# Attention opening and attention-to-experts hand-over of an LSH attention + MoE kernel: transfers, weight splits and their engines re-ordered

## The chip, the cores and the metric

One core of a Trainium2 chip runs the whole program. The metric is the device time of one execution in microseconds (us), the median over several executions. The kernel before takes 697.48 us (three runs, 697.29 to 697.70).

## The reference

Attention over 4 batches x 8 heads, 768 positions, head size 64, with a mask from locality-sensitive hashing; then a mixture of 8 experts over the 3072 x 512 result, one expert per token. All is fp32.

```
q_bits = einsum(q, proj) > 0 ; k_bits = einsum(k, proj) > 0        # 6 bits per position
mask   = (bucket(q_bits)[:, None] == bucket(k_bits)[None, :])
attn   = softmax(where(mask, q @ k.T / sqrt(64), -1e9)) ; o = attn @ v
x      = o as [3072, 512]
e      = argmax(x @ w_gate)                                        # top-1 of 8
y      = softmax(x @ w_gate)[e] * sigmoid(x @ w_output_gate)[e] * (relu(x @ w1[e]) @ w2[e])
```

w1[e] is 512 x 1024 and w2[e] is 1024 x 512.

## The kernel before, in words

**Precision.** Every fp32 product is made of three fp32r products: each operand is split into a high part (a rounding copy) and a low part (operand minus high part). A split is thus a copy and a subtraction, on VectorE, ScalarE or GpSimd (DVE, ACT and POOL in the rows), of every tile that TensorE (PE) multiplies: queries and keys (`qh`, `ql`, `kh`, `kl`), weights (`w1h`, `w1l`, `w2h`, `w2l`), tokens (`xh`, `xlo`).

**Attention.** 192 steps, 12 for each of 16 pairs of heads. A step makes a tile of 128 x 768 scores (`scores`, L600 to L615), its exponentials (`soft`, L623), scales it by the inverse row sum (`normal`, L626 to L633, two steps at a time, on GpSimd), transposes it on TensorE (`transposed`, L635 to L669) and, six steps later, multiplies it with the values (`weighted`, L671 to L683). `rows` (L685 to L699) turns the result and adds the routing products. The order of all engines' work, and of the transfers that SyncE (SP) issues, is written by hand there: `plan(step, ...)` puts a piece into a step, `block(step, when, ...)` around one. `late` is step 168 of 192; late + 24 is behind the last.

**Opening.** ScalarE issues two copies: 67 columns of the projection with thresholds (`pj`, L83), and 128 columns of signs (`signs`, L87 to L91), which `signed` (L93 to L95) multiplies on GpSimd to `pjc`. SyncE loads the queries and keys of four heads (`load`, L474), 128 x 768 each: first 384 columns and last 384. While these come, TensorE turns the identity 12 times (`turn_idle`, L1044 to L1046). `first_heads` (L513 to L551) then projects head 0 to its bits (L521), splits heads 0 and 1 and compares the projections (`bt`, L530 and L502), and `spread` copies bits and queries of head 1 across partitions by transfers (`spread_half` L575, `spread_bits` L581, `spread_bits_half` L587).

**Hand-over.** The first tokens of expert 0 are gathered while the last steps run (`early_gather`, L295, two indirect transfers of GpSimd by the list `gid`), turned and split. The four pieces of expert 0's w1 (`early_load`, L1007, through `load_weights`, L156 to L183) go into raw buffers `w_raw`, of which there are two: piece 2 takes the buffer of piece 0, and piece 3 that of piece 1. `early_w1` (L1011 to L1015) splits half a piece on GpSimd. Behind the last step come the second halves of pieces 2 and 3, then w2 of expert 0 in four pieces (`w2_piece`, L1133): two are read into the spare tile `pts0` of an attention block and have their high parts made on GpSimd and their lows on VectorE; two go through `w_raw` and have their high parts made on ScalarE and their lows on GpSimd. Between them TensorE runs the last `weighted`, the first layer of expert 0 in eight pieces (`fill`, L358, with `hl` L369 on VectorE) and the routing of the last 768 tokens: `add_pair` (L735, adds the last heads' gate products, from `ot`, L683), `best` (L741), `choose` (L743, L762), `prefix` (L797 to L802).

**Later experts** read their weights through four raw buffers in turn (two `w_raw`, `xh`, `xlo`).

## Time and profile before

| | |
|---|---|
| median of three runs | 697.48 us (697.29 to 697.70) |
| the profiled execution | 696.61 us |
| its span in the trace | 694.9 us |
| TensorE (PE) busy | 683.1 us, 98% of the span |
| VectorE (DVE) busy | 460.9 us, 66% |
| ScalarE (ACT) busy | 440.0 us, 63% |
| GpSimd (POOL) busy | 417.9 us, 60% |

The span is what the trace covers of the execution; 1.7 us lie around it. Busy time does not count waits, branches and the issuing of transfers. An engine that is idle costs something only where another one waits for it. PEld is TensorE's weight load, which overlaps its matmuls; a name with a q behind it (SPq) is a queue's issuing of transfers. `[0.84 <-POOL sc L633]` at a row's end says that the engine had been idle for 0.84 us, until GpSimd's instruction of line 633 released it.

### The profile page before, as it was taken

To read this page: it belongs to the slowest core of one execution; us is meant where nothing else is said; L and a number is where in the kernel's file an instruction comes from. 1 tells how busy PE (TensorE), PEld (TensorE's weight loads), DVE (VectorE), ACT (ScalarE), POOL (GpSimd) and SP (SyncE) were. 2 spreads that over 40 slices of the span, in tenths; PEclk is the share of its full clock that TensorE was granted. 3 is DMA by queue.
4 is the path that set the end of the run, shared out by engine and by line. 5 is a ranking of instruction groups with operands and counts; after the bars stand their busy time and mean duration, and the time that the engine had idled before them with its cause. 6 is when DMAs were issued, how large, how long until landed. Compare 5 with 4: busy or idle time off the path is not lost. (4 is left out here: it accounts for less than half of the span.)

```text
span 694.9 us, 17362 instructions
## 1 busy us (share of the span) xinstructions
PE 683.1 (98%) x6591; PEld 539.3 (78%) x6591; DVE 460.9 (66%) x1012; ACT 440.0 (63%) x896; POOL 417.9 (60%) x548
## 2 busy tenths in 40 slices
PE   8999999999999999999999999999999999999996
PEld 5667676767666766666666888889999999989896
DVE  7888887888887889788876934462536354556440
ACT  5988998889888988888986224433435252434231
POOL 6767766587856678657899447163372827374201
PEclk9999999999999999999999999999999999999999
DMA  5554554364444444443444136533455444535401
GB/s 175 150 129 98 129 130 97 75 141 112 110 118 99 117 99 121 99 99 73 134 112 139 34 122 207 208 109 117 142 167 167 164 159 165 171 126 212 153 11 44
DMA packets 85283, 87.47 MB, mean 126 GB/s; under 512 B 57167, under 2 KB 67591, under 8 KB 85192
## 3 DMA queue, kind: packets, MB, share of 16 engines
q1 hardware_dynamic: 79704, 72.88, 38.5%
q0 software_dynamic: 5200, 13.31, 5.8%
q8 instruction: 54, 0.88, 0.5%
q14 instruction: 37, 0.30, 0.1%
q10 hardware_dynamic: 288, 0.10, 0.1%
HBM read 59.57 MB, written 13.11 MB: 105 GB/s over the span
## 5 line engine op out<-in xcount | busy, mean ns | idle before, releaser
L633 POOL TENSOR_SCALAR sc<-sc,rsum 128x768 f32<-128x768 f32 x192 | 171.9, 911 | 79.9 <-ACT pts L669 40.2
L615 DVE TENSOR_SCALAR_CACHE_REDUCE sc<-ps_s 128x768 f32<-128x768 f32 x192 | 176.3, 955 | 24.1 <-PE ps_s L612 22.3
L623 ACT ACTIVATE sc<-sc,mn 128x768 f32<-128x768 f32 x192 | 178.9, 951 | 3.8 <-DVE sc L615 3.7
L612 PE MATMUL ps_s<-kh,qhl 64*128 64x384 f32 x768 | 148.2, 400 | 1.4 <-DVE sc L615 0.8
L680 PE MATMUL ps_a<-pts,vt 128*64 128x384 f32 x768 | 131.2, 490 | 0.0
L669 ACT COPY pts<-ps_t 128x384 f32<-128x384 f32 x188 | 93.0, 494 | 25.3 <-PE ps_s L662 22.0
L369 DVE SCALAR_TENSOR_TENSOR hl<-ps_s,hh 128x256 fp32r<-128x256 f32 (+8 forms) x40 | 34.0, 849 | 107.6 <-ACT hh L368 107.6
L680 PEld LDWEIGHTS ps_a<-pts,vt 128*64 128x64 f32 x768 | 52.5, 137 | 66.3 <-issue 60.9
L380 POOL DMA_INDIRECT out_dram<-yo,sid x29 | 30.7, 1059 | 113.9 <-ACT yo L375 52.2
L662 PEld LDWEIGHTS ps_t<-ident,sc 64*128 64x128 f32 x1140 | 81.9, 139 | 22.1 <-POOL sc L633 13.2
L358 PE MATMUL ps_s<-xh,w1h 128*128 128x256 f32 (+7 forms) x288 | 96.8, 336 | 0.4 <-DVE hl L369 0.4
L332 POOL DMA_INDIRECT xq<-x_dram,idx x75 | 82.2, 1096 | 23.8 <-issue 21.0
L358 PE MATMUL ps_s<-xlo,w1h 128*128 128x256 f32 (+7 forms) x288 | 95.4, 331 | 0.0
L358 PE MATMUL ps_s<-xh,w1l 128*128 128x256 f32 (+7 forms) x288 | 95.3, 331 | 0.0
L662 PE MATMUL ps_t<-ident,sc 64*128 64x64 f32 x1140 | 86.9, 223 | 1.3 <-POOL sc L633 1.3
L368 ACT ACTIVATE hh<-ps_s 128x256 fp32r<-128x256 f32 (+8 forms) x40 | 29.0, 726 | 90.4 <-PE ps_s L358 90.4
L612 PEld LDWEIGHTS ps_s<-kh,qhl 64*128 64x128 f32 x768 | 76.2, 187 | 4.4 <-DVE sc L615 2.2
L612 PE MATMUL ps_s<-kl,qhl 64*128 64x384 f32 x384 | 66.6, 333 | 0.0
L612 PE MATMUL ps_s<-bb 64*128 64x384 bf16 x384 | 65.3, 327 | 0.0
L669 ACT COPY pts<-ps_m 128x384 f32<-128x384 f32 x94 | 45.1, 480 | 17.5 <-PE ps_m L662 16.1
L358 PEld LDWEIGHTS ps_s<-xh,w1h 128*128 128x128 f32 x288 | 54.2, 188 | 2.3 <-issue 0.6
L358 PEld LDWEIGHTS ps_s<-xlo,w1h 128*128 128x128 f32 x288 | 54.2, 188 | 1.4 <-DVE xlo L315 0.2
(250 smaller groups left out, 1388.4 us busy)
## 6 DMA issues: line engine op xcount, KB each, us to landing
w_raw<-in_w_dram SPq DMA_DIRECT2D x34, 512.0 KB
qk<-in_qkT_dram SPq DMA_DIRECT2D x32, 384.0 KB
qhl<-qhl SPq DMA_DIRECT2D x62, 192.0 KB
xh<-in_w_dram SPq DMA_DIRECT2D x14, 512.0 KB
xlo<-in_w_dram SPq DMA_DIRECT2D x14, 512.0 KB
vt<-in_v_dram SPq DMA_DIRECT2D x16, 384.0 KB
x_dram<-xb SPq DMA_DIRECT2D x60, 96.0 KB
xq<-x_dram,idx POOLq DMA_INDIRECT x75, 3.0
```

The costliest lines, as they stand in the source:

```text
L332: nc.gpsimd.indirect_dma_start(out=xq[:, k * P:(k + 1) * P], out_offset=None, in_=x_dram.rearrange("n (a f) -> (n a) f", a=NB32), in_offse ...
L358: nc.tensor.matmul(ps, l, r, start=first and k == 0, stop=last and k == len(pairs) - 1)
L368: nc.scalar.activation(hh, ph, AF.Relu)
L369: return lambda: nc.vector.scalar_tensor_tensor(hl, ph, 0.0, f32(hh), ALU.max, ALU.subtract)
L380: nc.gpsimd.indirect_dma_start(out=out[:, :], out_offset=bass.IndirectOffsetOnAxis(ap=sid[0:n, r, a:a + 1], axis=0), in_=yo[0:n], in_offse ...
L612: nc.tensor.matmul(ss[:, h, 0:HS], q[rs, c:c + P], k[rs, 0:HS], start=(i == 0), stop=(i == 3))
L615: nc.vector.tensor_scalar(sc, ss[:, :, 0:HS], MASKED, None, ALU.min, ALU.min, accum_out=mn)
L623: nc.scalar.activation(pr, pr, AF.Exp, bias=mn, scale=-1.0, accum_out=sums[s // GROUP][:, k, 0:1])
L633: nc.gpsimd.tensor_scalar(live[s0 + k], live[s0 + k], rs[:, k:k + 1], 0.0, ALU.mult, ALU.add)
L662: nc.tensor.transpose(trs[h][:, c], pr[r, c * P:(c + 1) * P], ident[r, r])
L669: (nc.vector.tensor_copy if h and s and (last or s % PER == 0) else nc.scalar.copy)(pts[:, :, t * P + h * hq:t * P + (h + 1) * hq], trs[h])
L680: nc.tensor.matmul(st["av"][j * D:(j + 1) * D], st["v"][:, j, c], blocks[hb][j][:, c], start=(c == 0), stop=(c == NT - 1))
```

## The change

- Opening: `pj` and the signs come in one transfer of 195 columns, issued once by ScalarE. Head 0's queries and keys come in two transfers, last 384 columns first, and the projection begins with those. VectorE makes the low queries (`ql`) ahead of the comparison `bt`. Of head 1's spreading copies, one is issued by ScalarE, and the bits' copy of the second half comes first. TensorE turns the identity 9 times, not 12.
- Last steps: the split of w1's piece 1, second half, moves from step late + 14 to late + 18, behind the gathers; piece 3 is therefore read later (late + 18 for late + 15). The first half of piece 2 has its high part copied by ScalarE. The tile of step 184 is scaled by VectorE, not GpSimd.
- Behind the last step: all four pieces of w2 are read into the two spare tiles `pts0` and `pts1`. GpSimd makes the high parts of two, ScalarE of two, VectorE all four lows. The second halves of w1's pieces 2 and 3 are split behind w2's high parts, not ahead of them.
- As w2 of expert 0 no longer takes raw buffers, each later expert's pieces fall on the four raw buffers in another turn (first `w_raw`, `w_raw`, then `xh`, `xlo`).

GpSimd's order in the hand-over (instructions of its queue from the last piece of the step before the gathers on; `w1h`, `w1l`: half a piece of w1 split; `sc`: scaling; `w2h`, `w2l`: w2 split). Before:

```order
L1014 TENSOR_SCALAR w1h<-w_raw 128x512
L1015 TENSOR_TENSOR w1l<-w_raw,w1h 128x512
L633 TENSOR_SCALAR sc<-sc,rsum 128x768 x2
L295 DMA xg<-x_dram,gid_7521 128x512 x2
L633 TENSOR_SCALAR sc<-sc,rsum 128x768 x4
...
L633 TENSOR_SCALAR sc<-sc,rsum 128x768 x6
...
L180 TENSOR_SCALAR w2h<-pts_7897 128x1024 x2
L183 TENSOR_TENSOR w2l<-w_raw,w2h 128x1024 x2
```

Of the change, on the same engine and from the same place:

```order
L634 TENSOR_SCALAR sc<-sc,rsum 128x768 x2
L289 DMA xg<-x_dram,gid_7511 128x512 x2
L634 TENSOR_SCALAR sc<-sc,rsum 128x768 x3
L1018 TENSOR_SCALAR w1h<-w_raw 128x512
L1019 TENSOR_TENSOR w1l<-w_raw,w1h 128x512 x2
L1018 TENSOR_SCALAR w1h<-w_raw 128x512
L1019 TENSOR_TENSOR w1l<-w_raw,w1h 128x512
L634 TENSOR_SCALAR sc<-sc,rsum 128x768 x6
L174 TENSOR_SCALAR w2h<-pts_7889 128x1024 x2
...
L1019 TENSOR_TENSOR w1l<-w_raw,w1h 128x512
```

One split of w1 now stands behind the gathers, one scaling and one high part have left the queue, and two low parts of w2 are gone from its end, where two splits of w1 now stand behind w2's high parts.

VectorE behind the last step (`lgt`: gate logits, `xb`: turned rows, `ot`: the last heads' result, `hl`: low part of the first layer's result). Before:

```order
L727 TENSOR_REDUCE lgt<-ps_t 128x48
L183 TENSOR_TENSOR w2l<-pts_7897,w2h 128x1024 x2
L692 STREAM_TRANSPOSE xb<-ot 128x384
L736 TENSOR_TENSOR lgt<-lgt,ps_m 128x48
L683 COPY ot<-ps_a 128x384
```

Of the change:

```order
L728 TENSOR_REDUCE lgt<-ps_t 128x48
L177 TENSOR_TENSOR w2l<-pts_7889,w2h 128x1024 x2
L177 TENSOR_TENSOR w2l<-pts_7890,w2h 128x1024 x2
L693 STREAM_TRANSPOSE xb<-ot 128x384
L737 TENSOR_TENSOR lgt<-lgt,ps_m 128x48
L684 COPY ot<-ps_a 128x384
```

Four lows of w2 instead of two now stand ahead of `ot`.

VectorE in the opening, before:

```order
L527 TENSOR_TENSOR kl<-qk,kh 128x384
L530 TENSOR_SCALAR bt<-ps_m,pj 128x384
L531 SCALAR_TENSOR_TENSOR qhl<-qk,qhl 128x384
L502 TENSOR_SCALAR bt<-ps_a,pj 64x384
L544 SCALAR_TENSOR_TENSOR qhl<-qk,qhl 64x384
```

Of the change:

```order
L522 TENSOR_TENSOR kl<-qk,kh 128x384
L524 SCALAR_TENSOR_TENSOR qhl<-qk,qhl 128x384
L527 TENSOR_SCALAR bt<-ps_m,pj 128x384
L497 TENSOR_SCALAR bt<-ps_a,pj 64x384
L539 SCALAR_TENSOR_TENSOR qhl<-qk,qhl 64x384
```

The low queries and the first comparison have changed places. The diff:

```diff
--- before.py
+++ after.py
@@ -79,20 +79,14 @@
 
 
 
-    pj = cst.tile([P, D + 3], F32, name="pj")
-    nc.scalar.dma_start(pj, proj[:, 0:D + 3])
+    pj = cst.tile([P, D + 3 + 2 * D], F32, name="pj")
+    nc.scalar.dma_start(pj, proj)
     thr, scl, set0 = (pj[:, D + i:D + i + 1] for i in range(3))
     pjc = cst.tile([P, 2, 32], F32, name="pjc")
 
-    def signs():
-
-        t = gp.tile([P, P], F32, name="t_ob")
-        nc.scalar.dma_start(t, proj[:, D + 3:])
-        return t
-
-    def signed(t):
-
-        nc.gpsimd.tensor_tensor(pjc.rearrange("p m c -> p (m c)"), t[:, 0:D], t[:, D:P], ALU.mult)
+    def signed():
+
+        nc.gpsimd.tensor_tensor(pjc.rearrange("p m c -> p (m c)"), pj[:, D + 3:2 * D + 3], pj[:, 2 * D + 3:], ALU.mult)
 
     ident = cst.tile([P, P], F32, name="ident")
     wgt = cst.tile([P, H // 2, 32], F32, name="wgt")
@@ -471,7 +465,8 @@
             st.setdefault("qk", [])
             for j in heads:
                 t = hp.tile([P, S], F32, name="qk", bufs=4)
-                nc.sync.dma_start(t, qkT[2 * g + j])
+                for c in (slice(HS, S), slice(0, HS)) if g + j == 0 else (slice(0, S),):
+                    nc.sync.dma_start(t[:, c], qkT[2 * g + j, :, c])
                 st["qk"].append(t)
 
         def load_v(g):
@@ -510,26 +505,26 @@
                 st.setdefault(k, [None, None])[j] = hp.tile([P, HS], F32R, name=k) if t is None else t
             return (st[k][j] for k in ("qk", "qh", "ql", "kh", "kl"))
 
-        def first_heads(t):
+        def first_heads():
 
             qk, qh, ql, kh, kl = tiles(0, 0)
             qk1, qh1, ql1, kh1, kl1 = tiles(0, 1)
             bb = bits_of(0, 0)
             first = slice(0, HS)
             pp = ps_m.tile([P, HS], F32, name="ps_m")
-            for m in range(2):
+            for m in (1, 0):
                 nc.tensor.matmul(pp[m * D:(m + 1) * D], pj[:, 0:D], qk[:, m * HS:(m + 1) * HS], start=True, stop=True)
             nc.scalar.copy(kh, qk[:, KEYS])
             nc.vector.tensor_scalar(qh[DOWN, KEYS], qk[UP, first], -0.125, 0.0, ALU.mult, ALU.add)
             nc.scalar.activation(qh[:, first], qk[:, first], AF.Copy, scale=-0.125)
-            signed(t)
+            signed()
             nc.gpsimd.tensor_scalar(kh1, qk1[:, KEYS], 1.0, 0.0, ALU.mult, ALU.add)
             nc.vector.tensor_tensor(kl, qk[:, KEYS], f32(kh), ALU.subtract)
             nc.scalar.activation(qh1[:, first], qk1[:, first], AF.Copy, scale=-0.125)
+            nc.vector.scalar_tensor_tensor(ql[:, first], qk[:, first], -0.125, f32(qh[:, first]),
+                                           ALU.mult, ALU.subtract)
             bt = hp.tile([P, HS], BF16, name="bt", bufs=2)
             nc.vector.tensor_scalar(bt, pp, 0.0, set0, ALU.is_gt, ALU.is_equal)
-            nc.vector.scalar_tensor_tensor(ql[:, first], qk[:, first], -0.125, f32(qh[:, first]),
-                                           ALU.mult, ALU.subtract)
             for h in range(2):
                 r = D + 32 * h
                 nc.gpsimd.tensor_scalar(bb[h * D:h * D + 2 * NB, S:S + HS], bt[r:r + 2 * NB], 1.0, 0.0,
@@ -546,7 +541,12 @@
             nc.vector.scalar_tensor_tensor(ql1[:, first], qk1[:, first], -0.125, f32(qh1[:, first]),
                                            ALU.mult, ALU.subtract)
             nc.gpsimd.tensor_tensor(kl1, qk1[:, KEYS], f32(kh1), ALU.subtract)
-            spread(0, 1)
+            spread_bits_half(0, 1, 1, nc.scalar)
+            spread_bits(0, 1, 1)
+            spread_half(0, 1, 1)
+            spread_bits(0, 1, 0)
+            spread_half(0, 1, 0)
+            spread_bits_half(0, 1, 0)
             for x in (qh, ql):
                 nc.sync.dma_start(f32(x)[UP, KEYS], f32(x)[DOWN, first])
 
@@ -580,11 +580,11 @@
             r = 32 * (2 * j + m)
             nc.sync.dma_start(bb[rows, m * S:m * S + HS], bt[r:r + 4 * NB])
 
-        def spread_bits_half(g, j, h):
+        def spread_bits_half(g, j, h, e=nc.sync):
             bt, bb = pairs[g]["bt"], bits_of(g, j)
             up = FIRST + h * 2 * NB * EVERY
             r = 64 * j + (1 - h) * 2 * NB
-            nc.sync.dma_start(bb[up:up + 2 * NB * EVERY:EVERY, HS:S], bt[r:r + 2 * NB])
+            e.dma_start(bb[up:up + 2 * NB * EVERY:EVERY, HS:S], bt[r:r + 2 * NB])
 
         def spread(g, j):
             spread_bits(g, j, 1)
@@ -630,7 +630,8 @@
             nc.vector.tensor_reduce(rs, sums.pop(s0 // GROUP), AX.X, ALU.add)
             nc.vector.reciprocal(rs, rs)
             for k in range(GROUP):
-                nc.gpsimd.tensor_scalar(live[s0 + k], live[s0 + k], rs[:, k:k + 1], 0.0, ALU.mult, ALU.add)
+                e = nc.vector if s0 + k == NSTEP - PER - GROUP else nc.gpsimd
+                e.tensor_scalar(live[s0 + k], live[s0 + k], rs[:, k:k + 1], 0.0, ALU.mult, ALU.add)
 
         def transposed(s, pr):
             g, hf, t, j = tile_of(s)
@@ -1011,7 +1012,10 @@
         def early_w1(cc, h):
             c = slice(h * F // 2, (h + 1) * F // 2)
             hi, lo, raw = (x[:, c] for x in (*early["w1"][cc], early["raw"][cc]))
-            nc.gpsimd.tensor_scalar(hi, raw, 1.0, 0.0, ALU.mult, ALU.add)
+            if (cc, h) == (2, 0):
+                nc.scalar.copy(hi, raw)
+            else:
+                nc.gpsimd.tensor_scalar(hi, raw, 1.0, 0.0, ALU.mult, ALU.add)
             nc.gpsimd.tensor_tensor(lo, raw, f32(hi), ALU.subtract)
 
         plan(late + 2, compare, pick)
@@ -1020,15 +1024,12 @@
         for a in range(EARLY):
             block(late + 24, ("early", "amid")[a], lambda a=a: early_turn(a))
         for cc in range(NCC):
-            plan(late + (4, 5, 11, 15)[cc], lambda cc=cc: early_load(cc))
+            plan(late + (4, 5, 11, 18)[cc], lambda cc=cc: early_load(cc))
             for h in range(2):
-                if cc >= NCC // 2 and h:
-                    block(late + 24, "behind", lambda cc=cc, h=h: early_w1(cc, h))
-                else:
-                    plan(late + (9, 10, 13, 14, 18, 0, 20)[2 * cc + h], lambda cc=cc, h=h: early_w1(cc, h))
+                if cc < NCC // 2 or h == 0:
+                    plan(late + (9, 10, 13, 18, 19, 0, 20)[2 * cc + h], lambda cc=cc, h=h: early_w1(cc, h))
 
         with tc.manual_schedule(engines=MANUAL | {mybir.EngineType.SP}):
-            t = signs()
             load(0)
             load(1)
             for bb in halves[:2]:
@@ -1045,8 +1046,8 @@
                 for i in range(n):
                     nc.tensor.transpose(idle[:, i % 3], ident, ident)
 
-            turn_idle(12)
-            first_heads(t)
+            turn_idle(9)
+            first_heads()
             turn_idle(1)
             live = {}
             raw = []
@@ -1124,13 +1125,12 @@
                 lows.pop(0)()
 
             fill(0)
-            spare = tp.tile([P, NT, HS], F32, name="pts0").rearrange("p a b -> p (a b)")
-            pieces = {}
-            for f in (4, 6, 0, 2):
-                raw = spare[:, (f - 4) * DM:(f - 2) * DM].rearrange("p (f d) -> p f d", f=2) if f >= 4 else None
-                pieces[f] = w2_piece(ep, 0, f, "h" if f >= 4 else "l", raw)
+            spare = [tp.tile([P, NT, HS], F32, name=f"pts{n}").rearrange("p a b -> p (a b)") for n in range(2)]
             for f in range(0, NFB, 2):
-                w2s += pieces[f]
+                raw = spare[f // 4][:, f % 4 * DM:(f % 4 + 2) * DM].rearrange("p (f d) -> p f d", f=2)
+                w2s += w2_piece(ep, 0, f, "h" if f < 4 else "", raw)
+            for cc in (2, 3):
+                early_w1(cc, 1)
             for c in range(NT):
                 weighted(2 * NP - 1, c)
                 if c == 0:
```

## Rows read from the trace of the kernel before

**Rows 1.** Windows by stage: columns are us, each engine's busy us, PEclk, DMA share, GB/s

```profile
0.00:30.00 30.00, 26.53 (x251) 16.51 (x251) 23.00 (x57) 22.33 (x47) 21.06 (x33) 1.00 0.58 174
...
360.00:400.00 40.00, 37.07 (x385) 28.40 (x382) 29.82 (x92) 18.07 (x41) 28.89 (x30) 1.00 0.36 98
400.00:690.00 290.00, 289.68 (x1573) 269.66 (x1572) 135.07 (x146) 107.00 (x131) 130.23 (x131) 1.00 0.43 146
690.00:695.00 5.00, 0.00 (x0) 0.00 (x0) 0.00 (x0) 0.23 (x1) 0.92 (x1) 0.71 0.14 41
```

**Rows 2.** Timeline of the opening: start us, us, engine, line, operation [idle before <-releaser]

```profile
0.80 1.80 SPq L474 DMA_DIRECT2D qk<-in_qkT_dram  x4
...
4.12 0.51 ACT L522 CAST kh<-qk 128x384 fp32r<-128x384 f32 x1 [1.12 <-DMA qk<-in_qkT_dram]
4.31 0.30 PEld L521 LDWEIGHTS ps_m<-qk,pj 128*64 128x64 f32 x4 [0.46 <-DMA pj<-in_proj_dram]
...
5.91 0.62 DVE L530 TENSOR_SCALAR bt<-ps_m,pj 128x384 bf16<-128x384 f32 x1 [0.69 <-PE ps_m L521]
6.44 0.55 DVE L531 SCALAR_TENSOR_TENSOR qhl<-qk,qhl 128x384 fp32r<-128x384 f32 x1
...
8.37 1.25 DVE L546 SCALAR_TENSOR_TENSOR qhl<-qk,qhl 128x384 fp32r<-128x384 f32 x1
9.65 0.71 SPq L575 DMA_DIRECT2D qhl<-qhl  x1
```

**Rows 3.** Source lines 521 and 498: durations min/median/max in ns, first and last start

```profile
L521 PE MATMUL ps_m<-qk,pj x4: 847/874/902, 4.3 to 5.0; 128*64 128x384 f32 x4
L498 PE MATMUL ps_a<-qk,pjc x4: 487/513/543, 5.9 to 6.3; 128*32 128x384 f32 x4
```

**Rows 4.** Timeline of the last steps: gathers, scaling and w1 splits of POOL, and PE's wait

```profile
357.80 0.92 DVE L957 CAST gid<-o_gd 128x2 uint32<-128x2 f32 x1
360.66 1.21 POOL L295 DMA_INDIRECT xg<-x_dram,gid  x1 [0.19 <-issue]
363.18 3.55 POOL L633 TENSOR_SCALAR sc<-sc,rsum 128x768 f32<-128x768 f32 x4
364.15 0.27 PE L662 MATMUL ps_t<-ident,sc 64*128 64x64 f32 x1 [0.84 <-POOL sc L633]
366.71 0.62 POOL L1014 TENSOR_SCALAR w1h<-w_raw 128x512 fp32r<-128x512 f32 x1
367.41 1.28 POOL L1015 TENSOR_TENSOR w1l<-w_raw,w1h 128x512 fp32r<-128x512 f32 x1
370.63 5.31 POOL L633 TENSOR_SCALAR sc<-sc,rsum 128x768 f32<-128x768 f32 x6
376.35 0.59 PE L662 MATMUL ps_s<-ident,sc 64*128 64x64 f32 x12
```

**Rows 5.** Timeline behind the last step: a weight transfer's issue and its first use

```profile
377.92 2.28 SPq L173 DMA_DIRECT2D w_raw<-in_w_dram  x2
382.06 1.05 ACT L182 CAST w2h<-w_raw 128x1024 fp32r<-128x1024 f32 x1 [2.63 <-DMA w_raw<-in_w_dram]
```

**Rows 6.** Timeline behind the last step, w2's high parts, routing and PE's waits

```profile
379.80 2.05 POOL L180 TENSOR_SCALAR w2h<-pts 128x1024 fp32r<-128x1024 f32 x2
384.57 0.54 DVE L683 COPY ot<-ps_a 128x384 f32<-128x384 f32 x1
385.43 0.75 PE L735 MATMUL ps_m<-wgt,ot 128*128 128x32 f32 x6
389.95 0.20 PE L797 MATMUL ps_m<-ohb,tri 128*128 128x48 bf16 x1 [0.84 <-DVE ohb L762]
390.74 0.39 PE L358 MATMUL ps_s<-xh,w1h 128*128 128x256 f32 x1 [0.44 <-DVE hl L369]
```

**Rows 7.** Source lines 183 and 743 on VectorE and GpSimd: min/median/max in ns

```profile
L183 DVE TENSOR_TENSOR w2l<-pts,w2h x2: 1212/1628/2045, 380.9 to 382.8; 128x1024 fp32r<-128x1024 f32 x2
L183 POOL TENSOR_TENSOR w2l<-w_raw,w2h x2: 2390/2752/3115, 383.2 to 386.3; 128x1024 fp32r<-128x1024 f32 x2
L743 DVE TENSOR_TENSOR df<-lgt,mx x4: 207/209/1819, 136.3 to 386.9; 128x48 f32<-128x48 f32 x4
```

## The prediction, made before the changed kernel ran

> **What bounds the kernel.** I first read the windows by stage [rows 1]: TensorE is the engine to watch. From 400 us to 690 us it is idle for 0.32 of 290 us, and nothing on another engine can shorten that stretch. Its idle time sits in the first 30 us (3.47), in the last 40 us of the first part (2.93), and in the last 5, in which it has no work. The first two are what the change is about; all of them together, 6.4 us or 0.9% of the time, is more than it could ever gain. So I then read the timeline of these two stretches, and each time asked which engine ends TensorE's wait.
>
> In the opening the reader sees a chain [rows 2]: queries and keys are used at 4.12, the projection weights at 4.31 (the later of the two, and TensorE had then waited 0.46), the comparison `bt` runs at 5.91 when TensorE's four projections are out, VectorE is then without a pause until the low queries of head 1 (8.37 to 9.62), and the spreading transfer that waits for those is issued at 9.65.
>
> In the hand-over there are two kinds of waits. While the last steps run, GpSimd holds up TensorE: 0.84 us at 364.15, released by a scaling that stood behind the two gathers [rows 4]. Behind the last step VectorE does: 0.84 at 389.95 and 0.44 at 390.74 [rows 6]. The source views say why [rows 7]: `df` of line 743, 207 ns at its shortest, took 1819 ns at 386.90, and it ended at 388.7, just where the second low part of w2 on GpSimd ended (386.3 and the 2.39 of the shorter of the two). In the same view the low part of w2 on VectorE took 1212 ns once and 2045 ns once, the longer while GpSimd's two high parts still ran (379.80 and 2.05). VectorE's instructions with two SBUF inputs and GpSimd's hold each other up here, whole instruction by whole instruction.
>
> **The opening.** VectorE waited 0.69 us ahead of `bt` [rows 2]; `ql`, 0.55, fits into that gap, and then no longer stands between the two comparisons. What it gives is not all of 0.55, as the second comparison needs TensorE's next four passes: 6.8 instead of 7.02, so 0.2. Up to 0.65 more lies in the instruction at 8.37 (1.25 against 0.60 for its like), if GpSimd's neighbour no longer meets it. One transfer of 195 columns in place of 67 could land earlier or later than the 4.31 of before; the keys' half is half the bytes of what was used at 4.12, the low half is issued one place later. I take no gain there. The new issue order lets the transfer of head 1's queries start ahead of a bits copy; one issue is 0.45 (four in 1.80). I take **−0.4**, with ends −0.9 (0.2 and 0.65) and +0.3 (rival C). The three idle turns removed cost nothing as such.
>
> **The last steps.** Ahead of the gathers GpSimd loses one split (0.62 and 1.28, with the gap between them 1.98 [rows 4]). The gathers then wait for `gid` alone, written at 358.72 (0.92 long, much of it held by that very split), instead of 360.66. The pair takes 2.5 (to 363.18), so that the scalings begin at 361.2 and TensorE's 0.84 at 364.15 vanishes. VectorE's scaling of step 184 falls into a pause of that engine and costs nothing.
>
> But the split moved back has a load behind it. Piece 3 of w1 takes piece 1's buffer. Three scalings (0.89 each, 3.55 over four) end at 363.9, the split at 365.8, and only then can the load be issued. From issue to use took 3.32 in the opening (0.80 to 4.12) and 4.14 behind the last step (377.92 to 382.06 [rows 5]); I take the first, a lone load at a quiet queue, so 369.2, the other end 370.0. GpSimd has 1.28 of work until 367.1 and then **waits for about 2 us**. It splits piece 3 until 371.2, and the six scalings (5.31) end at 376.5, against 375.94 before. TensorE's last transposes stood 0.4 behind that end (376.35), so they come 0.1 to 0.5 later: **+0.3**. The 0.84 has been given back by the end of the stretch. Bounds: −0.84, if the load is much faster than any row, and +1.0 with 4.14.
>
> **Behind the last step.** The two low parts leave GpSimd (2.39 and 3.12 [rows 7]), `df` is not held, and 0.84 and 0.44 go: **−1.28**. In exchange VectorE makes four lows ahead of `ot`, and GpSimd has two splits of w1 to run beside them. GpSimd ends its high parts at 376.5 + 2.05 = 378.5, if w2 has come by then (it is read as soon as an attention block is done; with the longer of the two latencies it could be 0.9 late). Four lows are 4 x 1.21 = 4.85. If each of GpSimd's pieces gets in between two of them, that is 0.62, 1.28 and 0.62 more, so the last low ends at 385.9. Before, the second low started at 382.8 and ended at 384.0, and `ot` ended 1.1 behind that (384.57 and 0.54); now it ends at 387.0. TensorE wants it at 385.43 + 0.3 = 385.7 (`add_pair`, line 735 [rows 6]), where before it came just in time. So TensorE waits **+1.2** there, the new wait that takes the place of the old ones. Lowest 0, if the lows are not held; highest 3.4 (rival B).
>
> **Later experts.** The raw buffers are taken in another turn and expert 1's first loads go some 20 us earlier. TensorE had no wait there to lose; the transfers ran at 0.43 of their engines' time [rows 1]. I take 0, with +0.3 as the upper end, about the idle time that there is now.
>
> **Sum.** −0.4 + 0.3 − 1.28 + 1.2 = −0.2 us. On the profiled execution, 696.61, that is 696.4; the median of the runs stands 0.87 higher, 697.48, and the sum on it is **697.3**. 0.2% (1.4 us) is about what a measurement of this kernel can tell from no change, so the forecast is no change that can be told. Its own range, with the small ends of these terms, is 696.4 to 698.2.
>
> **Rivals.**
>
> A, the lows are not held. If VectorE's four lows run without a break, the last ends at 378.5 + 4.85 = 383.4 and `ot` at 384.5, over 1 us ahead of TensorE, and the 1.2 falls away: −1.4, so 696.1; with the opening at its best, 695.6. For it: VectorE's instructions stand one behind the other, so GpSimd may not get a turn. Against: the 2045 ns of the one low that met GpSimd. Chance 0.26.
>
> B, slower. GpSimd's pieces stand one behind the other as well; if it keeps its turn through the two splits of w1 (3.8 us to 382.3), the four lows end at 387.2 and `ot` at 388.2, a wait of 2.5, and with w2 0.9 late 3.4. The sum is −0.4 + 0.3 − 1.28 + 2.5 = +1.1, or +2.0: 698.6 to 699.5. It is slower by over 0.2% from where `ot` ends after 388.5. For it: `df` had to wait out GpSimd's whole second low. Against: it then went at once, at the instruction's end. Chance 0.14.
>
> C, the opening does not do what it says. With nine turns of the identity in place of twelve TensorE stands still for about 0.6 us before the projections. The same pass over 384 columns took 874 ns at 4.3 to 5.0 and 513 ns from 5.9 on [rows 3], though the granted clock is 1.00 over that stretch, the level of 2.4 GHz [rows 1]. If a gap there makes the later four passes as slow as the first, 2 x 0.36 = 0.7 go on the chain, and the opening is +0.3 for −0.4: +0.5, so 698.0. Chance 0.12. The Trainium skill speaks against removing the turns: its page "TensorE: Matmul & The Clock Gate", section "Part 1: The HAM clock gate (the "warmup" mystery)", has TensorE begin at half its clock and reach the full one by sustained activity. By that rule the time would be rival C's; the row of the durations speaks for it, that of the granted clock does not show it.
>
> **How the numbers follow.** The forecast has 0.48, A 0.26, B 0.14 and C 0.12. Faster by over 0.2% needs a time under 696.1: a bit over half of A (0.16) and the best ends of the forecast (0.04), so 0.20. Slower by over 0.2%, above 698.9, is most of B (0.10) and the far ends of the forecast and of C (0.04), so 0.14. The rest, 0.66, is no change. The range reaches into A and B until about a tenth on each side is out: 695.8 to 698.9.
>
> **What would show it.** In the changed trace: `ql` of head 0 ahead of `bt`, and the transfer of line 575's like issued ahead of 9.65; the gathers starting at about 358.7 and no wait of TensorE at 364; a wait of GpSimd of about 2 us for piece 3 of w1 near 367 to 369; six scalings ending after 376; four lows of w2 on VectorE with some over 1.8 us; `df` at 0.2 us; and a wait of TensorE for `ot` ahead of the second `add_pair`, of about 1.2. I am wrong about the last steps if GpSimd doesn't wait there, about the hand-over if the lows are all 1.2 us (A) or `ot` ends after 388 (B), and about the opening if TensorE's passes stay near 874 ns beyond the first four.

## The result, and the profile after

The changed kernel takes 702.68 us (six runs, 700.66 to 705.60), the kernel before 697.98 beside it (697.29 to 698.93): a ratio of 1.0071, 95% interval 1.0055 to 1.0087. It is **slower by 4.7 us**, where no change was forecast, and outside the range. Its profiled execution is the shortest of the six, 700.66 with a span of 698.9, 4.0 longer than the span before.

Windows of the changed kernel, columns us, TensorE's busy us, its clock, DMA share, GB/s. They answer to [rows 1], cut finer where the time went:

```profile
370.00:380.00 10.00, 8.04 (x98) 0.89 0.76 215
380.00:390.00 10.00, 10.00 (x68) 0.94 0.19 48
390.00:400.00 10.00, 10.00 (x86) 1.00 0.16 25
400.00:410.00 10.00, 9.17 (x43) 1.00 0.58 191
```

TensorE is idle for 2 us from 370 to 380 and 0.8 us in the 400s, where it had hardly waited. From 380 to 400 it does not wait at all any more. And its granted clock, 1.00 from 360 to 410 us before, is not 1.00: cut to 2 us, one stretch stands at 0.50, all of it at the 1.2 GHz level, behind two that have pauses:

```profile
374.00:376.00 2.00, 1.26 (x26) 1.00 0.71 229
376.00:378.00 2.00, 1.41 (x30) 0.95 1.09 334
378.00:380.00 2.00, 1.96 (x26) 0.50 0.88 340
380.00:382.00 2.00, 2.00 (x13) 0.69 0.39 154
```

The opening of the changed kernel in the timeline answers to [rows 2]. The first line here is of the kernel before, for head 1's tile; the others are of the changed kernel:

```profile
5.32 0.52 ACT L528 ACTIVATE qhl<-qk 128x384 fp32r<-128x384 f32 x1 [0.27 <-DMA qk<-in_qkT_dram]
...
3.54 0.51 ACT L517 CAST kh<-qk 128x384 fp32r<-128x384 f32 x1 [1.00 <-DMA qk<-in_qkT_dram]
5.75 0.62 DVE L527 TENSOR_SCALAR bt<-ps_m,pj 128x384 bf16<-128x384 f32 x1 [0.19 <-PE ps_m L516]
6.59 0.52 ACT L523 ACTIVATE qhl<-qk 128x384 fp32r<-128x384 f32 x1 [1.92 <-DMA qk<-in_qkT_dram]
6.70 0.84 PE L493 MATMUL ps_a<-qk,pjc 128*32 128x384 f32 x4 [0.99 <-DMA qk<-in_qkT_dram]
10.16 0.70 SPq L575 DMA_DIRECT2D qhl<-qhl  x1
```

Head 0's half is there early and `bt` runs 0.16 sooner, as forecast. But head 1's tile, used at 5.32 before, is used at 6.59, TensorE waits 0.99 for it, and the spreading transfer goes out 0.5 later than before.

The last steps and what follows, same view (issue queue, GpSimd, TensorE and VectorE; these answer to [rows 4, 6]; `xg` are the gathered tokens):

```profile
366.79 0.36 SPq L167 DMA_DIRECT2D w_raw<-in_w_dram  x1
371.22 0.62 POOL L1018 TENSOR_SCALAR w1h<-w_raw 128x512 fp32r<-128x512 f32 x1 [3.21 <-DMA w_raw<-in_w_dram]
373.18 5.33 POOL L634 TENSOR_SCALAR sc<-sc,rsum 128x768 f32<-128x768 f32 x6
374.15 0.59 PE L663 MATMUL ps_t<-ident,sc 64*128 64x64 f32 x12 [0.74 <-POOL sc L634]
380.41 2.77 DVE L177 TENSOR_TENSOR w2l<-pts,w2h 128x1024 fp32r<-128x1024 f32 x2
383.61 3.34 DVE L177 TENSOR_TENSOR w2l<-pts,w2h 128x1024 fp32r<-128x1024 f32 x2 [0.43 <-ACT w2h L176]
387.46 0.54 DVE L684 COPY ot<-ps_a 128x384 f32<-128x384 f32 x1
388.55 0.75 PE L736 MATMUL ps_m<-wgt,ot 128*128 128x32 f32 x6
390.02 0.21 DVE L744 TENSOR_TENSOR df<-lgt,mx 128x48 f32<-128x48 f32 x1
403.12 1.01 SPq L167 DMA_DIRECT2D w_raw<-in_w_dram  x2
409.94 0.72 PE L300 MATMUL ps_t<-ident,xg 128*128 128x128 f32 x4 [0.83 <-DMA xg<-x_dram,gid]
```

The load of w1's piece 3 leaves at 366.79 and is used at 371.22; GpSimd stands still for 3.21 us, its six scalings end at 378.5 instead of 375.9, and TensorE waits at each of five steps (0.74, then four times about 0.3). `df` runs at once. And expert 1's first two loads leave at 403.1, beside the gathers, whose second pair is then 0.83 late.

So that runs can be set side by side, this table gives how late TensorE is against the first profile of the kernel before: the start of one instruction less its start there, at six places (for the opening, ScalarE's and VectorE's instructions near 350 us). All in us.

| kernel | 350 | last transposes | second `add_pair` | 391, after `hl` | 410, after `xg` | 676 |
|---|---|---|---|---|---|---|
| changed | 0.7 | 2.2 | 3.1 | 1.5 | 2.5 | 2.6 |
| changed, again | 1.0 | 2.6 | 4.6 | 3.0 | 4.2 | 6.1 |
| before, again, same chip | -0.2 | -0.2 | -0.2 | -0.2 | -0.2 | 1.2 |

The last two lines stand side by side on one chip: the change costs 1.2 in the opening, then 3.6 until the second `add_pair`, wins 1.6 back at `df` and `hl`, and loses 1.2 at `xg`. Between 410 and 676, behind expert 0's second layer, it loses another 1.9. The kernel before loses 1.4 there in that run too, so that most of this step is not the change's.

In the first profile the last 1.4 of the 4.0 lie behind the last scatter (4.9 from its end to the end of the span, 3.5 before). That stretch was 3.5, 3.8 and 4.2 in three profiles of the kernel before, so it differs between executions. But on the same chip the kernels with a part of the change had more: 4.7 to 4.9 in three of them where the kernel before had 3.8, and 5.0 for the changed kernel where it had 4.2. So about 0.8 to 1.1 of a profile's difference lies behind the last instruction. Why is open.

### The profile page after: what moved, and what is told of

Its sections match the earlier page's. It is cut to its first block, busy times and chain, and to the rows that moved or that the text cites. A ratio compares the mean times of both kernels' runs of the same rounds, so it can differ in the third digit from the quotient of the medians.

```text
span 698.9 us, 17352 instructions
## 1 busy us (share of the span) xinstructions
PE 685.0 (98%) x6588; PEld 540.3 (77%) x6588; DVE 462.7 (66%) x1015; ACT 440.2 (63%) x897; POOL 416.0 (60%) x544
```

## The experiments

The runs were made on several chips, and the kernel before takes 697.4 to 700.2 us on them. So a run is compared by its ratio to the kernel before on its own chip, and two runs of different chips by their ratios. Each code excerpt shows the main lines of an edit and not all of them; "..." stands for what lies between.

**Parts alone or undone.** The opening of before put back into the changed kernel, and the new opening alone in the kernel before:

```diff
-    nc.scalar.dma_start(pj, proj)
+    nc.scalar.dma_start(pj, proj[:, 0:D + 3])
...
-                for c in (slice(HS, S), slice(0, HS)) if g + j == 0 else (slice(0, S),):
-                    nc.sync.dma_start(t[:, c], qkT[2 * g + j, :, c])
+                nc.sync.dma_start(t, qkT[2 * g + j])
...
-            turn_idle(9)
+            turn_idle(12)
```

> The changed kernel, with the opening of the kernel before whole (two copies by ScalarE, head 0 in one transfer, twelve idle turns, old order on VectorE and of the spreading copies). Theory (the new opening costs 0.5 us, because head 1's queries and keys land 1.3 us later behind the halves of head 0): the first tiles of scores come 0.5 us earlier (TensorE's passes that wait for the spread queries at 12.5 and not 13.0) and the median is 0.3 to 0.7 us lower, about 702.2. Rival (the opening as a whole is a gain and its loss is made elsewhere): no earlier or later than now.

702.19 us beside 699.13, ratio 1.0044 (1.0027 to 1.0060); at 350 it stands at 0.0. So what is lost ahead of 350 is the opening's, as the theory said. That the median meets the 702.2 is luck: by the ratios it is 1.9 us under the changed kernel, where 0.3 to 0.7 were expected. Its profile has something else to show. The load of w1's piece 3 was faster here:

```profile
366.10 0.36 SPq L173 DMA_DIRECT2D w_raw<-in_w_dram  x1
369.51 0.62 POOL L1018 TENSOR_SCALAR w1h<-w_raw 128x512 fp32r<-128x512 f32 x1 [2.19 <-DMA w_raw<-in_w_dram]
371.48 5.32 POOL L634 TENSOR_SCALAR sc<-sc,rsum 128x768 f32<-128x768 f32 x6
```

It took 3.41 from issue to use, and 4.1 to 4.6 in the five other profiles with that order. GpSimd waits 2.2, the scalings end at 376.8, the clock stays at 1.00 through four waits of 0.3, and TensorE is only 0.5 late at the last transposes.

> The kernel before with the new opening alone. Theory (head 1's queries and keys land over 1 us later, TensorE waits 1 us or more for them near 6 us, and its clock comes back later after that gap in many executions): 0.5 to 3.6 us at the first spread scores, the median 1 to 3 us above the kernel before, with a wider spread than its own. Rival (the gap only, no clock): 0.5 us above, within 0.3, with no wider spread.

698.56 beside 698.12, ratio 1.0006 (0.9992 to 1.0021); 0.7 late at 350 and to the end of TensorE's work. Nearer the rival: alone, the opening costs about half a us in the median, within the noise, and 1 us or more is not seen.

Head 0 in one transfer, the rest of the new opening kept:

```diff
-                for c in (slice(HS, S), slice(0, HS)) if g + j == 0 else (slice(0, S),):
-                    nc.sync.dma_start(t[:, c], qkT[2 * g + j, :, c])
+                nc.sync.dma_start(t, qkT[2 * g + j])
```

> The new opening alone, as in the run of the opening alone, but with head 0's queries and keys in one transfer as before (the merged copy of projection and signs, the order on VectorE and of the spreading copies, and the nine idle turns stay). Theory (the halving of head 0 is what puts head 1's queries and keys back): TensorE's wait of 1.0 to 1.2 us for head 1's queries and keys goes to under 0.3, and the first scores come 0.0 to 0.5 us earlier than in the kernel before instead of 0.4 later. Rival (the larger copy of the projection fills the queues and delays head 1): the wait stays at 0.8 or more.

700.92 beside 700.18, ratio 1.0006 (0.9992 to 1.0021). The wait for head 1 is gone, as the theory said: the halving delays head 1. But its first scores are not the 0.0 to 0.5 early that were expected, and the profile is 2.1 late at 350:

```profile
4.42 1.55 PE L515 MATMUL ps_m<-qk,pj 128*64 128x384 f32 x4 [0.82 <-DMA pj<-in_proj_dram]
5.90 1.49 PE L492 MATMUL ps_a<-qk,pjc 128*32 128x384 f32 x4
```

The projection starts at about its old time (4.31 before [rows 2]), and with three turns fewer TensorE now stands still ahead of it, for 0.82. The second four passes, fast before [rows 3], take 1.49 in all and are about as slow as the first four. This is what rival C of the prediction described. Slow passes go on to 13.7 us. But the run with two lows behind `ot`, which has the old opening with its twelve turns, shows the same in its profile and is 2.7 late at 350, so that the three turns are not shown to be the cause.

The last steps alone:

```diff
-            plan(late + (4, 5, 11, 15)[cc], lambda cc=cc: early_load(cc))
+            plan(late + (4, 5, 11, 18)[cc], lambda cc=cc: early_load(cc))
...
-                    plan(late + (9, 10, 13, 14, 18, 0, 20)[2 * cc + h], lambda cc=cc, h=h: early_w1(cc, h))
+                    plan(late + (9, 10, 13, 18, 19, 0, 20)[2 * cc + h], lambda cc=cc, h=h: early_w1(cc, h))
```

> The kernel before with the change to the last steps alone (gathers ahead of the split, piece 3 of w1 read later, one high part on ScalarE, step 184 on VectorE); opening, w2 and the turn of the raw buffers as before. Theory (GpSimd waits about 3 us for piece 3 and the six scalings pace TensorE): the scalings end 2 to 2.6 us later than before, TensorE's waits at 374 to 378 are back and perhaps the low clock, and the waits for df and hl behind the last step stay; the median 2 to 4 us above the kernel before. Rival (the late piece 3 is made good behind the last step, as the first run's 3.26 us with the piece in time suggests): within 1 us.

701.38 beside 698.12, ratio 1.0049 (1.0034 to 1.0064): the largest of the parts, though its interval meets that of w2. 0.3 late at 350, 1.9 at the last transposes, 4.2 at the second `add_pair`, 2.7 from 391 on. Unexpected was the 2.0 us of wait for `ot`, with w2 made as before: late scalings make w2's high parts late too, and they stand behind them on GpSimd.

w2 alone, in the old turn of the buffers:

```diff
+            spare = [tp.tile([P, NT, HS], F32, name=f"pts{n}").rearrange("p a b -> p (a b)") for n in range(2)]
+            for f in range(0, NFB, 2):
+                raw = spare[f // 4][:, f % 4 * DM:(f % 4 + 2) * DM].rearrange("p (f d) -> p f d", f=2)
+                w2s += w2_piece(ep, 0, f, "h" if f < 4 else "", raw)
+            for cc in (2, 3):
+                early_w1(cc, 1)
```

> The kernel before with the change to w2 alone (four loads into the spare tiles, all lows on VectorE, the two splits of w1 behind w2's high parts), and the old turn of the raw buffers. Theory (the four loads in a row take some 9 us to the last, so VectorE's third and fourth low end at 387 and ot with them, and TensorE waits about 2 us for ot; the 1.3 to 1.6 us of df are won back behind it): 0.3 to 0.8 us above the kernel before in the profile from 392 us on, the median within 1 us of it. Rival (the lows cost little and the gain is whole): 0.8 to 1.3 us faster.

701.05 beside 698.12, ratio 1.0032 (1.0016 to 1.0048): a loss, not within 1 us, and 2.8 late in the profile instead of 0.3 to 0.8. Its timeline (issue queue, ScalarE, VectorE):

```profile
374.85 2.05 SPq L163 DMA_DIRECT2D pts<-in_w_dram  x4
384.74 1.05 ACT L182 CAST w2h<-pts 128x1024 fp32r<-128x1024 f32 x1 [0.50 <-DMA pts<-in_w_dram]
385.82 1.35 DVE L183 TENSOR_TENSOR w2l<-pts,w2h 128x1024 fp32r<-128x1024 f32 x1 [0.20 <-ACT w2h L182]
387.68 0.54 DVE L683 COPY ot<-ps_a 128x384 f32<-128x384 f32 x1
```

The fourth load is used 9.9 us after the first left. `ot` stands behind it on VectorE, and TensorE waits 2.1 us. Windows of the same run (columns as above) show what the expectation had not priced: the clock falls behind that wait.

```profile
385.00:388.00 3.00, 1.13 (x10) 1.00 0.01 3
388.00:391.00 3.00, 2.73 (x15) 0.66 0.45 66
391.00:394.00 3.00, 3.00 (x27) 0.77 0.32 48
```

TensorE goes from 2.8 to 4.3 us late over passes that take 1.5 to 2 times as long. The wins at `df` and `hl` (1.4) then only pay for the clock.

**The split put back ahead of the gathers:**

```diff
-            plan(late + (4, 5, 11, 18)[cc], lambda cc=cc: early_load(cc))
+            plan(late + (4, 5, 11, 15)[cc], lambda cc=cc: early_load(cc))
...
-                    plan(late + (9, 10, 13, 18, 19, 0, 20)[2 * cc + h], lambda cc=cc, h=h: early_w1(cc, h))
+                    plan(late + (9, 10, 13, 14, 19, 0, 20)[2 * cc + h], lambda cc=cc, h=h: early_w1(cc, h))
```

> The changed kernel, with the split of w1's piece 1 (second half) put back ahead of the gathers and the load of piece 3 back to step late + 15; all else as changed. Theory (the load of piece 3, issued only behind that split, landed at 371.2 us, GpSimd waited 3.2 us for it, and its six scalings then paced TensorE and brought its clock down): GpSimd waits under 0.5 us there, the six scalings end at 376 to 377, the granted clock stays at 1.00 from 370 to 390, and the median falls by 2.5 to 4.5 us, to 698 to 700. TensorE's wait of some 0.8 us at 364 is back. Rival (the four lows of w2 on VectorE are what costs): the median stays above 701.5.

704.02 beside 699.13, ratio 1.0073 (1.0044 to 1.0102): no better than the change. The first theory falls as the whole cause. Its stages came as expected (1.0 late at the last transposes, clock 1.00), but the second `add_pair` is 3.15 late, as in the changed kernel. Its waits (us in total, times, longest):

```profile
PE ps_m L736 <- DVE ot L684: 1.9, 1, 1.9
PE ps_t L663 <- POOL sc L634: 1.6, 3, 1.1
```

Behind the wait for the scalings stood a second one, for `ot`, which the first had hidden.

**An own raw buffer for piece 3**, so that its load waits for no split: with the last steps alone, with the change to w2 too, and in the whole change:

```diff
+            own = wpool.tile([P, F], F32, name="w_own", bufs=1) if cc == 3 else None
...
-            plan(late + (4, 5, 11, 18)[cc], lambda cc=cc: early_load(cc))
+            plan(late + (4, 5, 11, 15)[cc], lambda cc=cc: early_load(cc))
```

> The change to the last steps alone, but piece 3 of w1 has a raw buffer of its own and is read at step late + 15, so that its load waits for no split; w2, opening and the buffers' turn as before. Theory (the load behind the moved split is the loss of the last steps): GpSimd's wait of over 3 us is gone, the six scalings end 1 to 2.5 us earlier than in the kernel before, TensorE's wait at 364 is gone and none comes at 374 to 378; its offset to the kernel before at 376 is -0.5 to -1.2 us, and the median 0.5 to 2 us under the kernel before. Rival (the gathers or the engine change are what costs): the offset at 376 stays above 1.

699.60 beside 700.18, ratio 0.9989 (0.9975 to 1.0002). From 0.25 early at 350 it gets to 1.8 early at the last transposes and keeps 1.6 of that to 410. Its six scalings begin at 368.96, where those of the kernel before begin at 370.63 [rows 4]:

```profile
368.96 5.32 POOL L634 TENSOR_SCALAR sc<-sc,rsum 128x768 f32<-128x768 f32 x6
```

The same last steps without the buffer had lost 1.6 there. So the load behind the split was the loss of the last steps. At 676 most of the gain is gone, by the step behind expert 0's second layer that the other profiles on that chip also show. The median is 0.6 lower, inside the theory's 0.5 to 2, but the interval does not exclude no change.

> As the run with piece 3's own buffer, and with the change to w2 as well (four loads into the spare tiles, all lows on VectorE), in the old turn of the raw buffers. Theory (the new w2 makes ot late by its four loads in a row and four lows, whatever the last steps do): TensorE waits 1.5 to 2.5 us for ot and loses it to the kernel with piece 3's own buffer alone by then; from 392 us on it stands 0 to 1.5 us behind that kernel. Rival (with GpSimd and the loads in time the lows fit and all of the 1.28 us is won): 0.8 to 1.3 us ahead of it.

700.30 beside 700.18, ratio 1.0005 (0.9992 to 1.0018). The wait for `ot` is 2.1; from 391 on it is 0.9 behind the run before. So the new w2 loses in the profiles with the old last steps and with these; in the medians the two runs are not told apart. The clock does not fall behind this wait, though it is as long as the one of w2 alone:

```profile
384.00:387.00 3.00, 0.95 (x9) 1.00 0.11 17
387.00:390.00 3.00, 3.00 (x31) 1.00 0.33 49
```

> The changed kernel whole, with a raw buffer of its own for piece 3 of w1, read at step late + 15. Theory (the load behind the moved split and ot behind the lows are two waits one behind the other, of which each shows when the other is gone): GpSimd's wait of 3.2 us is gone and the scalings end 2 us or more earlier than in the changed kernel, but TensorE waits about 2 us for ot; the offset from 392 on is 1 to 2.5 us lower than in the changed kernel, and the wait for xg stays; the median 1 to 2.5 us under the changed kernel, still at or above the kernel before. Rival (the buffer alone mends the change): at or under the kernel before by 1 us.

703.25 beside 697.41, ratio 1.0080 (1.0050 to 1.0110). The scalings are in time: 2.3 late at 350, it is 0.8 late at the last transposes. And still nothing is won: `ot` is waited for 2.2, the clock falls (0.89 and 0.77 from 385 to 395), `xg` is waited for 1.1. Two waits in a row were expected; that mending the first gains nothing at all was not.

**Lows behind `ot`**, both with the own buffer and the old opening: one of four with w2 read as before, two of four with the new w2 and the old turn of the raw buffers. Of the first:

```diff
             low()
+            nc.vector.tensor_tensor(lo2, raw2, f32(hi2), ALU.subtract)
             r["add_pair"](1, lp)
```

> The kernel with piece 3's own buffer (last steps changed, rest as before), and of w2's four lows two on VectorE ahead of ot as before, one on GpSimd, and one (of the second pair through the raw buffers) on VectorE behind ot and behind the first hl. Theory (df waits for GpSimd's second low, and ot for lows ahead of it, so a low between the two costs neither): no wait of TensorE for ot over 0.3 us, df at about 0.2 us, the wait for ohb under 0.5; TensorE's offset to the kernel before from 392 on is 0.5 to 1.1 us lower than that of the own buffer alone (-1.6), and the median 1.5 to 2.5 us under the kernel before. Rival (the low behind ot holds the routing chain by as much as GpSimd's did): within 0.3 us of the own buffer alone.

698.93 beside 697.41, ratio 1.0009 (0.9991 to 1.0027). Not won: the wait for `ot` is 1.9, and the clock falls behind it. VectorE and GpSimd in its timeline:

```profile
379.71 5.37 DVE L183 TENSOR_TENSOR w2l<-pts,w2h 128x1024 fp32r<-128x1024 f32 x2 [3.06 <-POOL w2h L180]
380.85 3.15 POOL L183 TENSOR_TENSOR w2l<-w_raw,w2h 128x1024 fp32r<-128x1024 f32 x1 [0.16 <-ACT w2h L182]
```

GpSimd's one low came earlier than before, between VectorE's two, and held the second: 5.37 for the pair against 1.21 each undisturbed [rows 7]. The Trainium skill, page "SBUF — State Buffer", section "Who interferes with whom", says that a VectorE instruction with two SBUF inputs and a GpSimd instruction that reads SBUF contend, for ports that are locked as a whole. The trace agrees, with the 5.37.

> The run with piece 3's own buffer and the new w2, with the lows of pieces 4 and 6 moved on VectorE from ahead of ot to behind ot and the first hl. Theory (the order makes ot late): the wait of 2.1 us for ot falls under 0.3; the two lows, 2.4 us, then stand ahead of the routing chain instead, and TensorE waits 0.5 to 1.5 us for ohb. Rival (GpSimd's pieces and the loads make ot late whatever stands ahead of it): ot still 1 us late or more.

697.37 beside 697.41, ratio 0.9999 (0.9980 to 1.0017). `ot` is no longer waited for (1.2 late at the second `add_pair`, as at the last transposes), and the two lows, 3.45 us, then hold `mx` and `ohb`: TensorE waits 1.2 in the middle of its first layer. From 350 to 391 it gains 1.1, and nothing of that is seen in the median. This run has none of the four losses of the change: the old opening, a load that waits for no split, an `ot` in time, the old turn of the raw buffers. It stands level with the kernel before.

**The raw buffers in the old turn:**

```diff
             lows = []
+            raws.extend((0, 1))
```

> The changed kernel, with the raw buffers of the later experts taken in the turn of the kernel before (expert 1 begins with xh). Theory (expert 1's first two loads, issued at 403.1 us, ran beside the gathers of expert 0's other tokens and made the second turn of tokens wait 0.83 us): no load of weights between 400 and 415 us, no wait of TensorE for xg, and the median 0.8 to 1.3 us lower, 701.4 to 701.9. Rival (the gathers are late because the stage ahead of them is, not by the loads): the wait stays at 0.6 or more and the time with it.

702.53 beside 699.13, ratio 1.0039 (1.0022 to 1.0056). No load beside the gathers, no wait for `xg`, 4.7 late at 391 and at 410 alike: as the theory said. Every run in the new turn lost 0.9 or more there, and none in the old. By the ratios the median is 2.2 us under the changed kernel, more than the 0.8 to 1.3 expected; on another chip, so how much of it is the turn's is open. This profile's opening is 3.6 late: the wait for head 1 is 1.3, and behind it passes of 384 columns that took 0.33 us before take 0.52 until 16.5 us. The window view still gives that stretch 1.00, but the trace holds no entry of the clock there: its first is at 16.59 us, and at 6.05 in the first profile of the kernel before. So the 1.00 ahead of these says nothing, and the passes' lengths have to tell.

**The clock.** Turns of the identity in TensorE's waits, in the last steps of the changed kernel and ahead of `add_pair` with w2 alone:

```diff
+            if behind in IDLE:
+                for _ in range(IDLE[behind]):
+                    nc.tensor.transpose(trs[0][:, 0:2].rearrange("p c q -> p (c q)"), ident, ident)
```

> The changed kernel, with turns of the identity on TensorE ahead of the transposes of the last steps (six ahead of step 186's, two ahead of each of the next four), into the same accumulators, which are overwritten. They fill TensorE's waits of 0.74 and four times 0.3 us. Theory (part of the loss is the clock, which was granted at 0.50 from 378 to 380 us and cost 1 us or more in passes that took 1.5 to 2 times as long): the granted clock stays at 1.00 through 370 to 390, and the median falls by 1 to 2 us, to 700.7 to 701.7, with a smaller spread. Rival (the clock's share is small, and the waits themselves are the loss): within 0.5 us of 702.7, or above.

703.77 beside 699.13, ratio 1.0062 (1.0040 to 1.0084). The clock stays at 1.00 from 370 to 390 and TensorE goes only from 2.1 to 2.5 us late there, where the changed kernel went from 2.2 to 3.1 and, again, from 2.6 to 4.6. But by the ratios the median is not told apart from the changed kernel's: `xg` is waited for 2.3, and the clock falls behind that. This run's opening shows the same fall in the record, behind a wait of 1.8 for head 1, while TensorE is busy all the time from 8 us on:

```profile
6.00:8.00 2.00, 0.95 (x5) 1.00 0.70 270
8.00:10.00 2.00, 2.00 (x12) 0.54 0.04 14
10.00:12.00 2.00, 2.00 (x13) 0.61 0.13 28
```

For the second, w2 alone with

```diff
             low()
+            more = ps_t.tile([P, 3, P], F32, name="ps_t")
+            for i in range(12):
+                nc.tensor.transpose(more[:, i % 3], ident, ident)
             r["add_pair"](1, lp)
```

> The change to w2 alone (as run before), with twelve turns of the identity on TensorE in the place where it waits for ot. They write an accumulator that nothing reads. Theory (1.4 of the 2.8 us that this part cost in its profile were the clock, granted at its lower level behind the wait of 2.1 us): the wait is filled, the granted clock stays at 1.00 from 385 to 400, TensorE's offset to the kernel before from 390 us on is 1.0 to 1.9 us in place of 2.9, and the median falls by 0.8 to 1.5 us against that run's 701.05. Rival (the clock would have come back alone in most executions): no lower than 700.7.

701.89 beside 700.18, ratio 1.0022 (1.0009 to 1.0036), against 1.0032 without the turns. Inconclusive: the twelve turns took 1.5 us, `ot` came 0.9 later than in the other run, 2.1 us of wait were left, and the clock fell behind them (0.50 from 390 to 395).

**Controls**, for what is not the change's:

> The kernel before, unchanged, profiled once more beside the next three. All theories: the same stages as in its first profile, with TensorE idle for 3.2 to 3.8 us in the first 30 us and 2.6 to 3.3 us from 360 to 400 us, no wait for xg, and head 1's queries and keys used before 5.6 us. If the waits of the changed parts show here too, they are not the change's.

696.97 us, span 695.3; the stages stand within 0.1 us of the first profile, and none of the waits of the changed kernel is there.

The kernel before with one idle turn less, and both kernels unchanged once more:

```diff
-            turn_idle(12)
+            turn_idle(11)
```

> The kernel before with eleven turns of the identity in place of twelve at the start, an edit that moves nothing else. Theory (the stretch behind the last instruction belongs to any edited program or to the execution, not to the change's parts): 4.2 us or more from the last scatter's end to the end of the span. Rival (it belongs to the parts of the change): 3.4 to 3.9 us as in the kernel before.

> The changed kernel once more. If the stretch behind the last instruction belongs to the program, it is 4.7 to 5.1 us again; if to the execution, it may be 3.5. The waits for head 1's queries and keys (about 1 us), of GpSimd for piece 3 (about 3 us), and for xg (about 0.8) are there again by the theory of the three places, whatever the clock does.

> The kernel before once more. If the stretch behind the last instruction belongs to the program, it is 3.4 to 3.9 us a third time; if to the execution, it may be over 4.2. None of the three waits of the changed kernel is there.

699.0, 704.34 and 698.52 us, one run each, beside 699.48 of the kernel before. Behind the last scatter lie 4.3, 5.0 and 4.2: the kernel before has more than its 3.5 and 3.8 this time, so the stretch varies with the execution, and the changed kernel still has 0.8 more on the same chip. The changed kernel again has all its waits: head 1 1.6, GpSimd 3.3, `xg` 1.0, and the clock is at 0.73 and 0.59 from 375 to 385.

## Why the prediction was wrong

**The opening**, -0.4, was +0.7 to +1.2 in the two profiles of the changed kernel. The step that failed is "the low half is issued one place later. I take no gain there". It looked at head 0 alone; what is issued later is every transfer behind it, and head 1's tile is on the chain. The gain ahead of it (`bt` 0.16 earlier, `ql` out of the way) came and was waited off. Rival C had the right sign, for another reason in these two profiles: their second four passes are fast, and the wait for head 1 is what costs. Its own mechanism, all four later passes as slow as the first, shows in two other profiles with the new opening, which are 2.3 and 3.6 late at 350, and in the one with head 0 in one transfer; but also in one of the twelve with the old opening. What brings it about is open. The 1.00 that the prediction held against it is no reading, as the run with the old turn shows.

**The last steps**, +0.3, were +1.5 to +1.6 at the last transposes in four profiles, and +2.4 to +3.6 with the clock and up to the second `add_pair` in those of the changed kernel. The mechanism was named: the load behind the split, GpSimd idle, the 0.84 given back. Mis-sized was above all the load's time (3.32 taken, 4.43 measured, above even the 4.14 of the bound). It was issued at 366.8 for 365.8, of which 0.7 is the opening's, and so the scalings ended at 378.5 for 376.5. In the one profile where the load took 3.41, the wait (2.2) and the end (376.8) are those of the working, and the cost is 0.5. The sum also let TensorE lose only what the last scaling loses; it waited at five of the six.

**Behind the last step**, -1.28 was -1.5 to -1.6: right. The wait for `ot`, +1.2, is not there in the changed kernel, since TensorE is late by more (388.55 against an `ot` done at 388.0). With the scalings in time it is 1.9 to 2.2, between the forecast and rival B, and it has a cause that the working did not have: four loads of 512 KB in a row, the last used 9.9 us after the first left. The working took one load's latency and "0.9 late" for all four. The hold-up by GpSimd that it did price came out smaller: the four lows took 6.1 us in the changed kernel, for 4.85 and 2.52 in the working.

**Later experts**, 0 with +0.3, was +1.0 to +1.2. "TensorE had no wait there to lose" was true and no argument: the gathers stood just ahead of need, and with the loads beside them they took 6.2 us from issue to landing in the median, for 3.4 before.

**The clock** was priced in the opening only. In the two profiles of the changed kernel a wait of 0.7 or 0.9 and several of 0.3 were followed by TensorE's lower clock, and 0.9 and 2.0 us more were gone; with w2 alone a wait of 2.1 was, and 1.5 were gone. But this is no rule. Of the seven profiles with a wait of 1.9 to 2.2 for `ot`, four have the lower clock behind it and three do not (last steps alone, the split put back, the own buffer with w2). The Trainium skill, page "TensorE: Matmul & The Clock Gate", section "HAM oscillation — how this bites in real kernels", tells of a kernel in which every pause for a load sends TensorE back to the lower clock. The windows above agree that a pause can do it, and differ in that not each one does. The six runs' mean clocks (0.993 to 0.998) do not go with their times, 702.43 at 0.998 and 702.67 at 0.993, so the clock does not explain the spread.

**The parts hide each other.** Alone they cost 0.06%, 0.49% and 0.32%, before the buffers' turn; the whole costs 0.71%. With these intervals the medians alone do not show that the sum fails. The stages do: the two large ones are waits on one chain, and with the first mended the wait for `ot`, which the changed kernel does not have, is there with 1.9 to 2.2 us.

## What to carry to other kernels

When a step is moved back, look for the load that waits for its buffer, and price it by the longest latency of that stage, with all the transfers that go with it; a moved or halved transfer delays everything behind it in the queue. When a wait is mended, ask which one stands right behind it: here mending the first alone, in the whole change, gained nothing measurable. And a wait of TensorE can cost more than its length, where the clock falls behind it. One profile of a kernel is one execution: the same load took 3.4 us in one and 4.6 in another, and the price of a stage is read from several.

## What the runs showed of the hardware

Four loads of 512 KB issued within 2.05 us were first used 3.5, 5.0, 7.9 and 9.2 us after the first left in one run (the split put back), the last 9.9 us after it in another (w2 alone). A single load of that size, issued alone in the last steps, was used after 3.4 to 4.6 us in six profiles. Behind a wait of TensorE of 2.1 us the granted clock was 0.66 and 0.77 in two stretches of 3 us (w2 alone), and 1.00 behind one of the same length in another run (own buffer with w2). In the run with one low behind `ot`, VectorE and GpSimd took turns one instruction at a time, so that a pair of VectorE's lows, 1.21 us each undisturbed, took 5.37. Gathers of tokens with two loads of 512 KB beside them took 6.2 us from issue to landing in the median, for 3.4 without (changed kernel and before).
